# First loads in halves on two queues, V of chunk 0 alone, and 1/std spread by products: one core, one kernel of attention and a gated MLP

## The chip, the cores and the metric

The kernel runs on 1 core of one Trainium2 chip. The metric is device time in microseconds (us) of one execution; lower is better. Every time below is a median of several executions, all of the fast state unless one is named. The profile is taken in one of these executions; its span is 1.7 to 2.1 us shorter than the time.

In the text, *step 0, 1, 2* are the first turns of the attention loop, *chunk 0 to 3* are the first four blocks of 128 tokens (together segment 0), *x0 to x3* their loads, and *PE* is the tensor engine. *Fills* are products of later projections that the kernel puts between the logits of a step. *Gates* are sigmoid(beta) for each head; the *mask* is made from them on GpSimd. A *row* of WV is 128 of its 1024 rows, what one product uses.

## The reference, cut to what matters

```python
x = A_x                                        # 2048 tokens x 1024, bf16
h = x + _A_ref(_layernorm(x), wq, wk, wv, wo, beta)   # 32 heads, 4 segments of 512 tokens
h2 = h + _B_ref(_layernorm(h), w_in, w_sp, b_sp, w_out)

# in _A_ref, for each segment s of 512 tokens:
q, k, v = x @ wq, x @ wk, x @ wv
a_dot = softmax(q k^T * scale + mask) v        # inside the segment
num, den = phi(q) @ M, phi(q) @ z              # memory of the segments before (none for s = 0)
o = g * num / den + (1 - g) * a_dot            # g = sigmoid(beta)
M, z = M + phi(k)^T v, z + sum(phi(k))
```

Only the start of `_A_ref` for segment 0 is touched: layer norm of chunks 0 to 3, their transposes, and the first Q, K and V.

## The kernel before

All engines run their own list of instructions in program order; a recorder puts semaphores where data depend on each other. For segment 0 the kernel centres each chunk (x minus its mean), transposes it on the PE, and applies 1/std only to the outputs: as a scale per partition for V, and as a row over all tokens (`RB`) for Q and K.

```python
for k in range(8):                       # all on SP: x0, x1, WV 0-1, x2, WV 2-3, x3, WV 4-5, WV 6-7
    if k in (0, 1, 3, 5): x_load((k + 1) // 2)
    else: ...                            # two rows of WV[0], 256 KB
sp.dma_start(WK[:, :, 0:256], ...)       # then beta, WQ[:, :, 0:256], WV[1]
...
act.activation(RDM[:, 0, 0:1], MHALF[:], ACTF.Exp)      # makes the table load happen early
dve.tensor_single_scalar(IDENT[:], IOT[:], 0.0, ALU.is_equal)
...
warm(9)                                  # 9 products of IDENT and zeros, to raise the PE's clock
act_mean(1)                              # ScalarE: Copy with accumulation
var0(ln_stats(XCH[0]))                   # VectorE: statistics of chunk 0
c0 = center(0, MV[0][:, 0:1], ALU.subtract)
c1 = center(1, MEAN[1][:])
pe_Th(0, c0, dve, dve); pe_Th(1, c1, act, dve)          # 8 transposes each, and the copies out
... # (cut) V of chunks 0 and 1 together, rows 0-3; chunk 2; rows 4-7; chunk 3
diag(0); v_out(0, 0, 0, vb[0]); diag(1); diag(2); diag(3)   # 1/std on diagonals, in two bf16 parts
v_out(0, 1, 0, vb[1])
proj_v(0, 2, 0)                          # V of chunk 2
gates(); mask_g()                        # sigmoid(beta), and a mask of it on GpSimd
bk, bq, br = next_bank(), next_bank(), next_bank()
mm8(bank(bk), WK..., XNT[0]...)          # K of step 0
for i in range(2):                       # a ones matrix times the diagonals: the row of 1/std
    pe.matmul(bank(br), ONES[:], DIAG[i][:]..., start=(i == 0), stop=(i == 1))
act.activation(RB[:], bank(br), ACTF.Copy)
qk_out(0, 1, bk)
mm8(bank(bq), WQ..., XNT[0]...)          # Q of step 0
qk_out(0, 0, bq)
for tc in range(4, 8): x_load(tc)
sp.dma_start(WK[:, :, 256:D], ...); sp.dma_start(WQ[:, :, 256:D], ...)
```

The softmax here doesn't subtract the row's maximum and nothing guards it: scores larger than these inputs give would overflow.

## Time and profile before

| | before |
|---|---|
| time, median of the first 3 executions | 796.65 us |
| span of the profile (an execution of 797.13) | 795.1 us |
| PE busy | 789.9 us, 99% |
| transposes of chunk 0 start | 6.10 us |
| V of chunk 2 starts | 12.31 us |
| first logits (step 0) start | 19.75 us |
| Q of step 2 starts | 30.11 us |

The page of the kernel before: busy time of each engine, and the chain that ended last.

```profile
PE 789.9 (99%) x5657; PEld 378.4 (48%) x5657; DVE 379.3 (48%) x745; ACT 295.6 (37%) x347; POOL 172.1 (22%) x329
...
PE 96%; DMA 2%; DVE 1%; ACT 0%; SPq 0%; issue 0%
```

The PE is the limit nearly everywhere. From 30 us on it has no wait worth naming, so a change of the head can only move the moment at which the PE gets through its first products. The four milestones in the table are such moments; the work of the PE between them is the same before and after, but for the spreading of 1/std (0.44 us of the PE before, 0.46 after).

The PE's timeline of the kernel before. Columns: start, busy time, engine, line, operation, output<-inputs, shape, count, and in brackets the idle time just before with what ended it.

```profile
1.74 4.02 PE L209 MATMUL ps<-etmp,ident 128*128 128x512 bf16 x9 [1.74 <-DVE ident L209]
6.10 1.14 PE L209 MATMUL ps<-ident,lno 128*128 128x128 bf16 x16 [0.34 <-DVE lno L209]
7.09 0.39 PE L209 MATMUL ps<-wv,xnT 128*128 128x512 bf16 x1
7.71 1.68 PE L209 MATMUL ps<-wv,xnT 128*128 128x512 bf16 x7 [0.23 <-ACT xnT L209]
9.68 0.62 PE L209 MATMUL ps<-ident,lno 128*128 128x128 bf16 x8 [0.29 <-DVE lno L209]
...
12.31 1.89 PE L209 MATMUL ps<-wv,xnT 128*128 128x512 bf16 x8
...
19.75 0.40 PE L209 MATMUL ps<-qk 32*128 32x512 bf16 x4
```

How to read the speed from such lines: a group of n products takes (n - 1) spacings and one product's own length (for 512 columns 0.38 us at full speed, 0.63 at half). Seven V products in 1.68 us are 216 ns apart, full speed. The nine warm-up products in 4.02 us are 427 ns apart, half speed. The Trainium skill, "TensorE: Matmul & The Clock Gate" (Part 1), says that the PE starts at half its clock and gets the full clock after about 3.4 us of activity, as judged in a free-running window of that length; the trace agrees with the two spacings, 427 and 216 ns. The warm-up is there for this: it ends at 5.76, 0.34 us before the first transposes, and V runs at full speed.

### The profile page before, as it was taken

The page shows a single profiled execution, that of the slowest core. Times are in us where ns is not written, and L with a number is a line of the kernel's source. Part 1 is how long each engine was busy: PE and PEld are TensorE (multiplying, and loading weights), DVE is VectorE, ACT ScalarE, POOL GpSimd, SP SyncE. Part 2 cuts the span into 40 slices and gives each one's busy share as a digit, 9 for nine tenths or more (in the row PEclk, how much of TensorE's full clock was granted, in tenths as well). Part 3 has the DMA queues.
Part 4 walks back from the last instruction along what each step waited for, and adds up shares of the span by engine and source line. Part 5 has one row for each costly group of instructions (what it writes and reads, how often), then busy time and mean ns, then how long its engine had stood idle before and what let it go on. Part 6 is the DMA issues. An engine that isn't in the chain of part 4 may idle for free.

```text
span 795.1 us, 13111 instructions
## 1 busy us (share of the span) xinstructions
PE 789.9 (99%) x5657; PEld 378.4 (48%) x5657; DVE 379.3 (48%) x745; ACT 295.6 (37%) x347; POOL 172.1 (22%) x329
## 2 busy tenths in 40 slices
PE   8999999999999999999999999999999999999998
PEld 3445455554554455455544444444444444444444
DVE  7664689679854766744562000053234323323332
ACT  5777877887787675133333333100000000000000
POOL 4564565565553331100230000000000000000000
DMA  9862555363415325411116000740270043011002
GB/s 292 181 162 57 94 81 121 87 105 84 107 23 125 114 67 139 121 47 54 54 54 132 1 1 0 222 90 7 79 133 1 33 109 78 1 59 54 1 7 86
DMA packets 125002, 64.83 MB, mean 82 GB/s; under 512 B 94992, under 2 KB 113936, under 8 KB 124944
## 3 DMA queue, kind: packets, MB, share of 16 engines
q1 hardware_dynamic: 124944, 63.99, 33.7%
q8 instruction: 44, 0.72, 0.4%
q14 instruction: 14, 0.11, 0.1%
HBM read 32.51 MB, written 8.39 MB: 51 GB/s over the span
## 4 chain that ended last, share of the span: by engine, by line
PE 96%; DMA 2%; DVE 1%; ACT 0%; SPq 0%; issue 0%
PE ps L209 96%; DMA wq<-in_A_wq_dram 2%; DMA xch<-in_A_x_dram 0%; DVE stats L209 0%; ACT junk L209 0%; DVE xnT L209 0%; DVE lno L209 0%; SPq L209 0%; ACT xnT L209 0%; DVE mv L209 0%; DVE fin L209 0%
## 5 line engine op out<-in xcount | busy, mean ns | idle before, releaser
L209 PE MATMUL ps<-wspT,z 128*128 128x512 bf16 x896 | 194.0, 379 | 0.0
L209 ACT ACTIVATE e<-ps 128x2048 bf16<-128x2048 f32 (+1 forms) x96 | 152.6, 1590 | 41.9 <-PE ps L209 41.8
L209 PEld LDWEIGHTS ps<-wspT,z 128*128 128x128 bf16 x896 | 87.7, 98 | 105.7
L209 DVE TENSOR_TENSOR tmpg<-ps,brow 128x512 f32<-128x512 f32 x56 | 38.7, 691 | 196.7 <-DMA brow<-in_B_b_sp_dram 104.0
L209 POOL TENSOR_SCALAR_AFFINE_SELECT e<-e 128x512 bf16<-128x512 bf16 x128 | 90.4, 718 | 127.2 <-ACT e L209 127.1
L209 PE MATMUL ps<-win,hnT 128*128 128x448 bf16 x512 | 98.3, 352 | 0.0
L209 PE MATMUL ps<-w_out,yT 128*128 128x512 bf16 (+2 forms) x462 | 97.4, 373 | 0.0
L209 PE MATMUL ps<-hnT,win 128*128 128x512 bf16 x448 | 96.9, 379 | 0.0
L209 PEld LDWEIGHTS ps<-win,hnT 128*128 128x128 bf16 x512 | 49.7, 98 | 46.4 <-issue 0.2
L209 PEld LDWEIGHTS ps<-w_out,yT 128*128 128x128 bf16 x462 | 44.7, 98 | 52.3
L209 PEld LDWEIGHTS ps<-hnT,win 128*128 128x128 bf16 x448 | 43.8, 98 | 52.8
L209 PE MATMUL ps<-xnT,wk 128*128 128x512 bf16 x256 | 60.8, 380 | 0.0
L209 PE MATMUL ps<-xnT,wq 128*128 128x512 bf16 x256 | 60.6, 379 | 0.1
L209 PE MATMUL ps<-wv,xnT 128*128 128x512 bf16 x256 | 59.4, 380 | 0.2 <-ACT xnT L209 0.2
L209 ACT ACTIVATE z<-ps 128x448 bf16<-128x448 f32 x60 | 32.5, 543 | 69.4 <-PE ps L209 69.4
L209 PE MATMUL ps<-wo,oT 128*128 128x512 bf16 x256 | 58.0, 379 | 0.0
L209 ACT ACTIVATE z1T<-ps 128x512 bf16<-128x512 f32 x56 | 33.4, 597 | 63.3 <-PE ps L209 63.3
L209 DVE TENSOR_TENSOR fin<-fin,ps 128x512 bf16<-128x512 bf16 (+2 forms) x33 | 22.2, 671 | 71.2 <-DMA fin<-out_dram 39.7
L209 DVE BATCH_NORM_STATS2 zst<-z 128x6 f32<-128x448 bf16 x64 | 38.9, 619 | 30.1 <-ACT z L209 30.1
L209 PEld LDWEIGHTS ps<-v,e 128*128 128x128 bf16 x1280 | 38.8, 96 | 14.0 <-issue 6.5
L209 PE MATMUL ps<-v,e 128*128 128x33 bf16 x1280 | 42.2, 178 | 0.0
L209 DVE TENSOR_TENSOR yT<-tmpg,z1T 128x512 bf16<-128x512 f32 x56 | 38.8, 692 | 1.9
(86 smaller groups left out, 609.3 us busy)
## 6 DMA issues: line engine op xcount, KB each, us to landing
xch<-in_A_x_dram SPq DMA_DIRECT2D x16, 256.0 KB, 3.3
xr<-in_A_x_dram SPq DMA_DIRECT2D x16, 256.0 KB, 3.7
out_dram<-hch SPq DMA_DIRECT2D x16, 256.0 KB, 2.4
fin<-out_dram SPq DMA_DIRECT2D x16, 256.0 KB, 2.8
out_dram<-fin SPq DMA_DIRECT2D x31, 128.0 KB, 1.7
win<-in_B_w_in_dram SPq DMA_DIRECT2D x4, 896.0 KB, 5.1
w_out<-in_B_w_out_dram SPq DMA_DIRECT2D x1, 3584.0 KB, 12.7
win<-in_B_w_in_dram SPq DMA_DIRECT2D x3, 1024.0 KB, 5.2
```

The source lines that it names most:

```text
L209: ins = getattr(e, op.name)(*op.args, **op.kw)
```

## The change

Its intent: get the PE to work on chunk 0 sooner. x0 and x1 are loaded in halves, one half by SP and one by ScalarE's queue, in step with single rows of WV. The mean of chunk 0 is taken in two halves on two engines. V of chunk 0 runs alone instead of in pairs with chunk 1. The diagonals on VectorE go; the row of 1/std comes from eight small products whose stationary operand is one column of 1/std repeated with step 0. The warm-up no longer waits for the identity. Gates and mask move behind Q and K of step 0, and the fills of step 0 are rearranged; one background piece of layer norm in step 2 (`bg_pop`) also moves behind a fill, which the cut below leaves out.

```diff
-    for k in range(8):  ... (all on SP, whole chunks; see above)
+    for kind, k in (("x", 0), ("w", 0), ("w", 2), ("x", 1), ("w", 4), ("w", 6)):
+        for h, eng in ((0, sp), (1, act)):
+            if kind == "x":
+                x_half(k, h, eng)            # 128 KB
+            else:
+                wv_row(k + h, eng)           # 128 KB
+    x_load(2)
+    x_load(3)
...
-            pe.matmul(bank(7), IDENT[:], ETMP[:, 0, :], start=True, stop=True)
+            pe.matmul(bank(7), ETMP[:, 0, 0:128], ETMP[:, 0, :], start=True, stop=True)
...
-    warm(9)
-    act_mean(1)
-    var0(ln_stats(XCH[0]))
...
+    warm(8)
+    act_half(0)                              # ScalarE: half of the sum
+    dve_half(0)                              # VectorE: the other half, and both together
+    center_half(0, 0)
+    center_half(0, 1)
+    pe_Th(0, LNO[0], dve, dve)
+    act_mean(1)
+    v_pair(0, 0, 6)                          # V of chunk 0 alone
...
+    stats0(0, 0)  ... act_var(1) ... act_var(2) ... stats0(3, 0) ...   # statistics later
+    dve.tensor_copy(RSB[:, 0, :], RSW[:, :, 0])
+    dve.tensor_tensor(RSB[:, 1, :], RSW[:, :, 0], RSB[:, 0, :], ALU.subtract)
...
-    gates()
-    mask_g()
...
-        pe.matmul(bank(br), ONES[:], DIAG[i][:].rearrange("p c n -> p (c n)"), start=(i == 0), stop=(i == 1))
+    for t in range(4):
+        for h in range(2):
+            pe.matmul(PS[:, br, t * 128:(t + 1) * 128], RSB[:, h, t:t + 1].to_broadcast([128, 128]), IDENT[:],
+                      start=(h == 0), stop=(h == 1))
...
+    gates()
+    mask_g()
```

## The prediction

> **What bounds the kernel.** The page gives the tensor engine (PE) 789.9 of 795.1 us busy, and the chain of waits is 96% PE. In the PE timeline the first warm-up product starts at 1.74 us and the last product ends near 792.8, so all PE gaps sum to about 1.2 us. From 30 to 140 us no PE group waits 0.15 us. The change touches only the first 30 us, so it can gain only earlier first logits (19.75 us now) plus those gaps: a ceiling of about 1.5 us, 0.2%.
>
> **What the head looks like now** (timeline, landings in the trace). x0 lands at 3.83, x1 4.45, x2 7.42, x3 8.80 us; pairs of WV rows at 6.08, 8.12, 9.54, 10.32. Chunk 0 pays two statistics reads (1.42), an aggregate (0.21) and a centring (0.49), so its transposes start at 6.10. From 7.7 the PE runs almost solid: gaps of 0.23 us and 0.29 us.
>
> **Costs of the change.**
> - Chunk 0's mean: half a Copy with accumulation on ScalarE (whole one 1.06 + 0.19; a half about 0.63 + 0.19) beside a half reduction on VectorE (est. 0.6), a tiny combine (0.2), one half-centring (0.27): about 1.4 us from landing to first transpose instead of 2.25, a possible 0.8 us.
> - Against it: ScalarE must issue six DMAs (0.43-0.47 us each on SP's queue, 2.7 us) beside its table load (1.28). Serial, ScalarE is free only at 0.8 + 2.7 + 1.3 + 0.2 = 5.0 us and transposes start near 6.1, no gain; overlapped, near 4.9.
> - x1 moves behind four WV rows, x2 and x3 to the very end. x1 becomes the end of the first 1 MB (was 512 KB): about 6.2-7.2, x3 about 9.3-10.3. ScalarE's means are serial (1.25 each), so chunk 3's transposes cannot start before x3 + 1.25 + 0.45 + 0.1, or 11.1-12.1; now 11.86. This likely eats the early start.
> - Two queues: rate dips to 234-300 GB/s between 3.5 and 7 us, against 350-385 later. The Trainium skill ("DMA: Bandwidth & Descriptors", Issuing engines are not separate DMA queues) says a second issuer saves only issue time; the dip leaves room for about 1 us at most.
> - Spreading 1/std: eight 0.60-us-per-pair VectorE diagonal operations vanish (2.4 us of VectorE, off the critical path); two 512-column products (0.43 us) become eight 128-column ones (est. 8 x 0.06 = 0.5): zero or slightly worse for PE.
> - Gates and their mask move about 3.4 us later on GpSimd (5.8 us of work, now 16.5 to 22.3, then to about 25.7); four selects then end near 28.4, just when the first value products (28.4) need them: little or nothing.
>
> **Sum.** Chunk 2's value products, now from 12.31 us, start at 11.7-12.6; PE work from there to the first logits is unchanged (7.35 us needed, 7.44 taken). Net -0.5 us, from -1.4 to +0.4.
>
> **Predicted:** 796.1 us, 8 in 10 between 795.2 and 797.0. Faster by over 2%: 0.005; within 2%: 0.99; slower by over 2%: 0.005.
>
> **What would show it.** Right: span about 794.6, PE busy share still 99%, first transposes at 4.9-6.1, a PE wait for chunk 1 or 2 data between 6 and 11 us, logits of step 0 at 19.0-20.0, the same spacing after 30 us. The supply step is wrong if x3 lands before 9 us; the ScalarE step is wrong if its first half-mean starts before 4.
>
> **What would make it wrong.** The PE staying at the cold spacing (427 ns per 512 columns) after a shorter warm-up; a mask on GpSimd arriving late and stalling the first value products.

## More of the kernel before

One more line of before, from VectorE's timeline, is needed later: the add of phi of K in step 0.

```profile
18.73 0.28 DVE L209 TENSOR_SCALAR pqk<-qk 128x512 bf16<-128x512 bf16 x1
```

## The result

| | before | after |
|---|---|---|
| time, median of 6 executions each | 796.70 us | 798.86 us |
| span of the profile | 795.1 us | 797.1 us |
| PE busy | 789.9 us | 790.8 us |
| transposes of chunk 0 start | 6.10 | 6.47 |
| transposes of chunk 2 start | 9.68 | 12.10 |
| V of chunk 2 starts | 12.31 | 13.86 |
| first logits start | 19.75 | 21.77 |
| Q of step 2 starts | 30.11 | 32.25 |

The ratio of the times is 1.0029 with a 95% interval of 1.0016 to 1.0042. Ratios here are the mean time of one kernel's fast runs over that of the other's of the same rounds, so not quite the ratio of the medians quoted. The change costs about 2.2 us: small, within 2%, but clear of noise and outside the predicted range.

The milestones say where. 1.55 us are lost ahead of V of chunk 2; 0.47 more up to the first logits (7.91 us instead of 7.44 from V of chunk 2); 0.12 more up to Q of step 2 (10.48 instead of 10.36; the changed kernel loses 0.59 us there, shown below, but the kernel before also lost time there that the changed one does not, mainly 0.28 us ahead of Q of step 2 for the load of WQ). The difference of the spans is 2.0 us. Nothing is lost after about 25 us.

Two cautions. First, the profile of before is one of its slower executions (797.13 us). In g2 below, whose head is that of before, the profile is of a usual one (796.45): there x2 landed at 6.28 instead of 7.42, V of chunk 2 starts at 11.93 and the first logits at 19.36. Against that the head of the changed kernel loses 1.93 us and 2.41 us, not 1.55 and 2.02. Second, time minus span is 2.0 to 2.1 us in every execution of before, f3 and g2 whose span is on record, and 1.7 to 1.8 in every such execution of the kernels with the new spreading, f2 too. So about 0.3 us change outside the span, where no timeline shows them; no run says why.

The page of the changed kernel, the same two lines:

```profile
PE 790.8 (99%) x5662; PEld 378.3 (47%) x5662; DVE 378.8 (48%) x741; ACT 296.3 (37%) x349; POOL 170.0 (21%) x328
...
PE 97%; DVE 1%; ACT 1%; POOL 0%; ACTq 0%; issue 0%; DVEq 0%
```

These whole-kernel numbers say almost nothing about the loss; PE's busy share is 99% in both. The PE's timeline of the changed kernel does:

```profile
1.24 3.37 PE L209 MATMUL ps<-etmp 128*128 128x512 bf16 x8 [1.24 <-DVE etmp L209]
6.47 0.66 PE L209 MATMUL ps<-ident,lno 128*128 128x128 bf16 x8 [1.86 <-DVE lno L209]
7.38 2.51 PE L209 MATMUL ps<-wv,xnT 128*128 128x512 bf16 x6 [0.26 <-DVE xnT L209]
9.69 1.06 PE L209 MATMUL ps<-ident,lno 128*128 128x128 bf16 x8
...
12.10 0.61 PE L209 MATMUL ps<-ident,lno 128*128 128x128 bf16 x8
...
13.86 1.89 PE L209 MATMUL ps<-wv,xnT 128*128 128x512 bf16 x8
...
18.63 0.62 PE L209 MATMUL ps<-ident,rsb 128*128 128x128 bf16 x8 [0.29 <-DVE rsb L209]
...
21.77 0.40 PE L209 MATMUL ps<-qk 32*128 32x512 bf16 x4
22.10 1.90 PE L209 MATMUL ps<-wv,xnT 128*128 128x512 bf16 x8
24.42 0.61 PE L209 MATMUL ps<-xnT,wq 128*128 128x512 bf16 x2 [0.41 <-DVE qk L209]
```

Four things are to be seen. First, the PE idles 1.86 us between the warm-up and the first transposes. Second, the six V products from 7.38 take 2.51 us, where at full speed they would take 1.46 (5 x 0.216 + 0.38), and the eight transposes from 9.69 take 1.06 us instead of 0.61: the PE has fallen back to half speed, from about 7.6 to 11.0 us by the starts of the products. Such a group shows no idle time and counts as busy; only its length for its count gives it away. (The last warm-up product was already short, so the full clock had come at about 4.2 us.) Third, there is a wait of 0.29 us for the new 1/std columns. Fourth, there is one of 0.41 us for an output of K, ahead of Q of step 1.

Why chunk 0 is late is in ScalarE's timeline of the changed kernel (ACTq is its queue of loads):

```profile
0.79 0.40 ACTq L209 DMA_DIRECT2D xch<-in_A_x_dram  x1
...
2.67 0.94 ACTq L209 DMA_DIRECT2D wv<-in_A_wv_dram  x2
3.64 1.28 ACT L209 ACT_TABLE_LOAD   x1 [3.64 <-issue]
4.93 0.20 ACT L209 ACTIVATE rdm<-mhalf 128x1 f32<-128x1 f32 x1
5.04 0.61 ACT L209 ACTIVATE junk<-xch 128x512 bf16<-128x512 bf16 x1
...
9.97 1.06 ACT L209 ACTIVATE junk<-xch 128x1024 bf16<-128x1024 bf16 x1 [1.50 <-DMA xch<-in_A_x_dram]
```

ScalarE issues its six loads until 3.6 us, and only then does its first activation bring the table load, 1.28 us (the Trainium skill, "ScalarE: Activation LUTs", What ACT_TABLE_LOAD costs, states about 1283 ns; the trace agrees). The half mean of chunk 0 starts at 5.04, 1.2 us after both halves are there. The last line shows the supply side: chunk 2's mean starts when x2 lands, at 9.97; before, it started at 7.55.

The fourth wait shows on VectorE and GpSimd in the changed kernel's timeline:

```profile
21.75 1.05 POOL L209 COPY maskg<-gs 128x1024 f32<-128x1024 f32 x1 [3.57 <-DVE gs L209]
...
21.81 1.13 DVE L209 TENSOR_SCALAR pqk<-qk 128x512 bf16<-128x512 bf16 x1
```

The add of phi of K takes 1.13 us instead of 0.28, and it ends 0.14 us after GpSimd's copy ends. The Trainium skill, "SBUF — State Buffer" (Who interferes with whom), says that VectorE in its fast modes and GpSimd hold one pair of ports exclusively and the later one is blocked for the whole instruction. The trace fits: the later one was VectorE's add. With the gates moved, VectorE makes this add just when the mask's first copy runs.

### The profile page after: what moved, and what is told of

Read it like the earlier page. It is cut to its first block, busy times and chain, and to the rows that moved or that the text cites. A ratio compares the mean times of both kernels' runs of the same rounds, so it can differ in the third digit from the quotient of the medians.

```text
span 797.1 us, 13128 instructions
## 1 busy us (share of the span) xinstructions
PE 790.8 (99%) x5662; PEld 378.3 (47%) x5662; DVE 378.8 (48%) x741; ACT 296.3 (37%) x349; POOL 170.0 (21%) x328
## 4 chain that ended last, share of the span: by engine, by line
PE 97%; DVE 1%; ACT 1%; POOL 0%; ACTq 0%; issue 0%; DVEq 0%
PE ps L209 97%; ACTq L209 0%; POOL rsw L209 0%; DVE qk L209 0%; ACT junk L209 0%; DVE pqk L209 0%; ACT L209 0%; POOL rs L209 0%; ACT rb L209 0%; ACT xnT L209 0%; DVE gs L209 0%; DVE xnT L209 0%; DVE lno L209 0%; DVE rsb L209 0%; DVE fin L209 0%
```

## The experiments

The theory after the result: (A) ScalarE's late start lets the PE idle, and this costs it its full clock; (B) x2 and x3 now land late; (C) the statistics and 1/std come late; (D) the late gates block VectorE. The rivals: all of the first part is supply, or the order of V, or the step-0 operand is slow. Each batch of kernels ran on one chip with runs of the kernel before beside it; the ratios are against these. Each ratio has an interval of about 0.0012, or 1 us, to either side, and the changed kernel itself came at 798.86 us in its first batch and at 798.45 in a later one (r1). Smaller differences between two repaired kernels are therefore read from the milestones in the traces, one profile each, and not from the times. (Expectations for e1 and its batch name 6.77 us and 7.9 to 11.4 us; I had read these with a zero 0.3 us too late. In the profile they are 6.47 and 7.6 to 11.0.)

### e1: fourteen warm-up products

```diff
-    warm(8)
+    warm(14)
```

> The changed kernel with 14 warm-up products instead of 8, so that the PE is fed until the first transposes (6.77 us). Clock theory: the half-speed stretch seen from 7.9 to 11.4 us (427 ns between 512-column products) vanishes; chunk 2's transposes start near 11.7 instead of 12.10, V of chunk 2 near 13.4 instead of 13.86, time 0.3 to 0.6 us under the changed kernel's 798.86. Supply theory (ScalarE free at 5.0, x1 at 7.25, x2 at 9.89, x3 at 10.60 us set the pace alone): spacing becomes 216 ns but V of chunk 2 stays within 0.15 us of 13.86 and the time within 0.2 us.

Measured: 797.85 us (before beside it: 796.56), ratio 1.0012, 1.0 us under the changed kernel's first batch and so more than I expected. V of chunk 2 at 12.99 instead of 13.86. The warm-up stayed at half speed, lasted to about 7.2 and pushed the first transposes from 6.47 back to 7.19, and still the head ended 0.87 us sooner, because every product after it was 216 ns apart. This speaks for the clock, but x2 landed 0.6 us earlier in this profile than in the changed kernel's, so the size was not settled; r1 and r2 below settle it.

### e2: the loads of before

```diff
-    for kind, k in (("x", 0), ("w", 0), ("w", 2), ("x", 1), ("w", 4), ("w", 6)): ...
-    x_load(2)
-    x_load(3)
+    for k in range(8): ...                   # as before: all on SP, x1 second
```

> The changed kernel with the loads of before: whole chunks, one queue (SP), x1 before the WV rows; everything else of the change stays. Supply theory: ScalarE starts its half mean at x0's landing (3.8) instead of 5.04, transposes of chunk 0 start near 5.0, V of chunk 2 near 12.0 to 12.4 (now 13.86), and 1.3 to 1.9 us come back: about 797.2. If the order of V (chunk 0 alone) is what costs: V of chunk 2 stays after 13.2 and under 0.7 us comes back. The waits after it (0.4 for 1/std, 0.4 for the late mask) should stay if they are not consequences of the late start.

Measured: 797.91 us where about 797.2 was expected, ratio 1.0020; one of its six executions took 800.94. Transposes at 5.03, no half-speed stretch, V of chunk 2 at 12.83: better than the change, not as good as expected. The PE's timeline of e2 shows the new wait:

```profile
7.18 0.60 PE L209 MATMUL ps<-wv,xnT 128*128 128x512 bf16 x2 [0.64 <-DMA wv<-in_A_wv_dram]
8.68 0.59 PE L209 MATMUL ps<-wv,xnT 128*128 128x512 bf16 x2 [0.89 <-DMA wv<-in_A_wv_dram]
```

V of chunk 0 alone eats rows of WV twice as fast as the pair of chunks does, and with the old order of loads it waits for them. So the new order of loads and V of chunk 0 alone belong together; neither can be judged without the other. The two later waits (0.29 and 0.41 us) stayed, as expected.

### e3: the table load first

```diff
+    pool.memset(MHALF[:], -0.5)
+    act.activation(RDM[:, 0, 0:1], MHALF[:], ACTF.Exp)
     for kind, k in (("x", 0), ("w", 0), ...        # the loads; the two lines above moved up from below
```

> The changed kernel with the warm-up Exp (and so its table load) issued on ScalarE ahead of its six loads. If the table load and the issues overlap: table load at 0.8 to 2.1, the loads issued in the same time, half mean at 3.8, transposes of chunk 0 near 5.0 to 5.3 instead of 6.47, the PE idle under 0.5 us before them, no half-speed stretch; time 0.4 to 0.8 us under 798.86. If they are serial whatever the order: ScalarE's first load is issued only near 2.2, x0 lands near 5, nothing gained (within 0.2 us).

Measured: 798.01 us, ratio 1.0014, 0.85 us under the change's first batch and 0.44 under r1, which ran on the same chip. ScalarE's timeline of e3:

```profile
0.79 1.28 ACT L209 ACT_TABLE_LOAD   x1 [0.79 <-PEq L970]
0.93 0.38 ACTq L209 DMA_DIRECT2D xch<-in_A_x_dram  x1
...
3.77 0.63 ACT L209 ACTIVATE junk<-xch 128x512 bf16<-128x512 bf16 x1 [1.48 <-DMA xch<-in_A_x_dram]
```

Table load and issues overlap when the load comes first. The half mean starts at 3.77, the transposes at 5.21, no product after them is at half speed, and V of chunk 2 starts at 12.50. With one line moved, most of the first loss is gone in this profile; x2 also landed 1.0 us earlier in it than in the changed kernel's first (8.92 against 9.89), which the table under r1 and r2 takes apart. The 0.3 and 0.4 us waits stayed.

### e4: the gates back

```diff
+    gates()
+    mask_g()
     bq, br, bk = 5, 6, 7
     ...
-    gates()
-    mask_g()
```

> The changed kernel with the gates and their mask back ahead of K of step 0, as before the change. Gates theory: GpSimd does the mask from about 16.5 to 22.5 instead of 21.75 to 27.3; the add for phi of K (1.04 us on VectorE in the changed kernel, 0.28 before) is short again, the 0.41 us PE wait ahead of Q of step 1 (24.42 us) vanishes, time 0.3 to 0.5 us lower. Rival (the wait is from the order of the step-0 fills): the wait stays and the time is within 0.15 us. The three gate operations of VectorE in front of the 1/std rows could cost up to 0.3 us at the spreading instead.

Measured: 798.18 us, ratio 1.0018. The wait ahead of Q of step 1 is gone (PE's timeline of e4):

```profile
22.03 1.90 PE L209 MATMUL ps<-wv,xnT 128*128 128x512 bf16 x8
23.76 0.59 PE L209 MATMUL ps<-xnT,wq 128*128 128x512 bf16 x2
```

From V to Q are 1.73 us, where the change took 2.32 (22.10 to 24.42): 0.59 us. The phi add fell from 1.13 to 0.52 us. V of chunk 2 (13.77) and the wait for 1/std (0.31) stayed. Theory D holds.

### f1: three repairs in the changed kernel

The table load first, the gates back, and chunk 0's statistics right after its copies, where VectorE is idle:

```diff
     pe_Th(0, LNO[0], dve, dve)
+    stats0(0, 0)
+    stats0(0, 1)
+    aggr0(0)
     act_mean(1)
```

> The changed kernel with three repairs at once: the table load ahead of ScalarE's loads, the gates back ahead of K of step 0, and VectorE's statistics of chunk 0 done in its idle time after chunk 0's copies instead of behind chunk 3's centring. If the loss is the sum of these waits: no half-speed stretch, V of chunk 2 near 12.5, the idle PE before the spreading products 0 to 0.1 us instead of 0.29, no wait before Q of step 1; the first logits near 20.0 to 20.2 (21.77 in the changed kernel, 19.75 before) and the time about 796.4 to 797.0, level with before. If something else in the change costs (the order of the loads, the step-0 fills): over 797.4.

Measured: 796.92 us (before beside it: 796.58), ratio 1.0005 with an interval of 0.9992 to 1.0017: level with before. First logits at 20.41 rather than the hoped 20.0 to 20.2; no half-speed stretch and no wait ahead of Q of step 1. The wait for 1/std became smaller but did not vanish: from the first product of Q of step 0 to the spreading are 1.10 us (16.16 to 17.26), in the changed kernel 1.32 (17.31 to 18.63), where four products take 0.86. By the times these waits make up about 1.8 of the 2.2 us. In the profile less is mended: the first logits are still 0.66 us later than in the profile of before, and V of chunk 2 came near 12.7 (its first product is missing from the trace) instead of 12.5. Part of the early start is spent on loads: the PE idled 0.68 us ahead of the fifth V product, whose row of WV landed at 7.71, and 0.56 us ahead of chunk 1's transposes (the second half of x1 landed at 7.19). No gain is shown for what remains of the change.

### f2: only the new spreading, in the kernel before

```diff
-    diag(0) ... diag(3);  pe.matmul(bank(br), ONES[:], DIAG[i][:]...)
+    (two small VectorE operations; eight products with RSB[:, h, t:t + 1].to_broadcast([128, 128]))
```

> The kernel before with only the new spreading of 1/std (eight 128-column products with a stationary operand of step 0, two small VectorE operations, no diagonals). Theory: the products with step 0 cost no more than others (56 ns apart, weight loads of 98 ns) and the spreading can start a little earlier, as the pair of diagonal operations behind the last 1/std (0.6 us) becomes 0.35 us: first logits 0.05 to 0.25 us earlier than 19.75, time within 0.3 us of before. Rival (the step-0 operand loads slowly or small products cost much): over 100 ns apart, first logits 0.3 us or more later.

Measured: 796.26 us, ratio 0.9998 (0.9986 to 1.0011). PE's and PEld's lines for the new operand in f2:

```profile
L209 PEld LDWEIGHTS ps<-ident,rsb x8: 97/98/98, 15.1 to 15.7; 128*128 128x128 bf16 x8
L209 PE MATMUL ps<-ident,rsb x8: 219/219/219, 15.4 to 15.7; 128*128 128x128 bf16 x8
```

The columns in the middle are least, median and greatest duration in ns. A weight load from one repeated column takes 98 ns like any other, and the eight products take 0.61 us as a group, as eight transposes do. From K to Q of step 0 are 2.17 us, before 2.16. The first logits came at 19.35, but in this profile the transposes of chunk 0 also started earlier, at 5.76; in g2, which starts at 5.79 and keeps the old spreading, the first logits came at 19.36. So the hoped 0.05 to 0.25 us did not come. Inside the span the spreading is neutral, and the rival of a slow step-0 operand falls.

### f3: only the late gates, in the kernel before

```diff
-    gates()
-    mask_g()
     ...
     qk_out(0, 0, bq)
+    gates()
+    mask_g()
```

> The kernel before with only the gates and their mask moved behind the outputs of Q and K of step 0, as the change has them. Theory: the mask on GpSimd then runs beside VectorE's phi of K, whose add grows from 0.28 to about 1.0 us, and K of step 1 is taken out of its bank late; before, Q of step 1 follows a whole V and the same banks, so 0.3 to 0.6 us are lost between the first logits and 28.4 us: time 0.2 to 0.6 us over before. Rival (the move only hurts together with the new step-0 fills): within 0.15 us of before.

Measured: 797.08 us against 796.58, ratio 1.0005 with an interval of 0.9992 to 1.0019, so not clear by time. In the profile the phi add takes 1.13 us here too, and from the first logits to K of step 2 are 7.15 us instead of 6.92. The block on VectorE comes with the move alone; how much of it reaches the PE depends on the fills (0.59 us in the new ones, about 0.2 in the old).

### f4 and g1: a mix of both kernels

f4 takes the loads of before, the half means of the change, V by pairs of rows as WV lands, statistics in idle time, early gates and the new spreading. The core of the edit to the changed kernel:

```diff
-    v_pair(0, 0, 6)  ... v_pair(0, 6, 8) ... v_pair(1, 0, 4) ... v_pair(1, 4, 8)
+    v_pair(0, 0, 2); (chunk 1's transposes); v_pair(1, 0, 2); v_pair(0, 2, 4); v_pair(1, 2, 4)
+    (chunk 2's transposes); v_pair(0, 4, 6); v_pair(1, 4, 6); (chunk 3's); v_pair(0, 6, 8); v_pair(1, 6, 8)
```

> A new mix: the loads of before (one queue, x1 ahead of the WV rows), chunk 0's mean in two halves as in the change, the V products of chunks 0 and 1 row pair by row pair in the order in which WV lands, the statistics in idle time, gates early, the new spreading. Theory (ScalarE's late start, the supply order and V of chunk 0 alone were the losses, the half means and the spreading are sound): transposes of chunk 0 near 5.0, V of chunk 2 at 11.6 to 12.1 (12.31 before), first logits at 19.0 to 19.5, time 0.3 to 0.9 us under before. If it is not under before, the half means buy nothing because WV's landing (last pair near 10.3) sets the pace.

Measured: 796.22 us, ratio 0.9997 (0.9984 to 1.0009). The head came out as expected (transposes at 4.96, first logits at 19.35), but PE's timeline of f4 shows where it was given back:

```profile
30.46 1.67 PE L209 MATMUL ps<-xnT,wq 128*128 128x512 bf16 x7 [1.08 <-DMA wq<-in_A_wq_dram]
```

(Seven of the eight products are in the trace. If the first is the missing one, the wait was about 0.87 us.) Q of step 2 needs columns of WQ that come in the last of the early loads, and in this profile these landed at 30.11 us, although the PE was early. In the kernel before, Q of step 2 started at 30.11, right after the same load. g1 splits these loads:

```diff
-    for tc in range(4, 8): x_load(tc)
-    sp.dma_start(WK[:, :, 256:D], ...); sp.dma_start(WQ[:, :, 256:D], ...)
+    sp.dma_start(WK[:, :, 256:512], ...); sp.dma_start(WQ[:, :, 256:512], ...)
+    for tc in range(4, 8): x_load(tc)
+    sp.dma_start(WK[:, :, 512:D], ...); sp.dma_start(WQ[:, :, 512:D], ...)
```

> The mix of f4 with the rest of WK and WQ loaded in two parts: columns 256 to 511 of each ahead of chunks 4 to 7 of x, the other half behind them. In f4 the PE waited 1.08 us for the end of the WQ load (landed 30.1 us) before Q of step 2. Theory: that wait was the only place where f4's early start was given back; it vanishes, Q of step 2 starts near 29.4, span near 794.0, time 0.7 to 1.3 us under before. Rival (other waits take its place, as the same bytes must land by then): time no better than f4's 796.22.

Measured: 796.10 us, before beside it 796.52, ratio 0.9991 (0.9979 to 1.0004). The wait is gone, Q of step 2 starts at 29.13, the span is 794.0: as foreseen. The time gained is 0.4 us by the medians, half of what I expected, and 0.7 by the ratio; about 0.3 of it lies outside the span. All five executions (795.66 to 796.27) lie below all nine of before (796.34 to 797.34), but the interval still touches 1. I had compared with the profile of before, an execution of 797.13; its usual execution is about 0.6 us faster.

### g2: the same split in the kernel before

The edit is the split of g1, and nothing else.

> The kernel before with only the same split of the later WK and WQ loads. Its Q of step 2 starts at 30.11, right when the WQ load lands (30.06). Theory: 0.1 to 0.3 us come back; this is also the amount that hides part of any loss or gain of the head in before. Rival: within 0.1 us.

Measured: 796.45 us, ratio 1.0001: nothing, so the rival holds. In its profile Q of step 2 starts at 29.45. In before, the WQ load is only in the way in some executions: in f2, with the same later loads as before, it landed at 28.32 and nothing waited for it.

### g3: f1 with all first loads on one queue

```diff
-        for h, eng in ((0, sp), (1, act)):
+        for h, eng in ((0, sp), (1, sp)):
```

> f1 with its first loads in the same order and sizes, but all issued by SP instead of half by ScalarE. If two queues only save issue time: SP needs 16 issues of 0.45 us (7 us), so x2 and x3 are issued near 6 us and land at most 0.5 to 1.5 us later than in f1 (9.1 and 9.9 us); chunk 0's halves land within 0.5 us of f1; the time is within 0 to 0.8 us above f1's 796.92. If two queues do not matter at all: within 0.2 us. If two queues raise the rate of the first MB: x1 lands over 1 us later than 7.2.

Measured: 798.69 us, 1.8 us over f1 (on another chip; 2.0 by the two ratios to before), ratio 1.0030: far outside what I expected. SP's timeline of g3:

```profile
3.61 0.91 SPq L209 DMA_DIRECT2D xch<-in_A_x_dram  x2
4.56 1.85 SPq L209 DMA_DIRECT2D wv<-in_A_wv_dram  x4
6.45 0.91 SPq L209 DMA_DIRECT2D xch<-in_A_x_dram  x2
```

One issue takes 0.46 us, and with 131,072 bytes each that caps a single queue at about 285 GB/s, an estimate (131,072 bytes over 0.46 us). x2 and x3 are issued only at 6.45, and in this profile, which fell on a slow execution (800.75; the others took 798.4 to 798.9), the PE waited 2.89 us for chunk 2 (x2 landed at 11.56, in f1 at 9.13) and then ran at half speed again, from about 13.9 to 17.3. x1 landed at 6.30 and 6.64, no later than in f1 (6.99 and 7.19), so two queues are not shown to raise the rate of the first loads. So halves need the second queue. It does not follow that halves on two queues beat whole chunks on one: with those, in before, x3 landed at 8.80 and the last WV pair at 10.32; after the change the last WV row landed at 9.17 and x3 at 10.60.

### r1 and r2: the changed kernel again, and eleven warm-up products

r1 has no edit. r2:

```diff
-    warm(8)
+    warm(11)
```

> The changed kernel itself once more, beside the next one on the same chip, to see what of its head repeats. Expected if the half-speed stretch belongs to the kernel: 3 us or more of products spaced 427 ns (512 columns) or 107 ns (128 columns) after the first transposes again, V of chunk 2 at 13.6 to 14.0, time 798.3 to 799. If the stretch of the first profile was luck of that run: products 216 ns apart from 7.4 us on, V of chunk 2 near 13.2. Whole chunk 2's landing, 9.89 in the first profile, tells how much of the start of V is load luck.

> The changed kernel with 11 warm-up products: at 427 ns they end at 5.9, 0.5 us before the first transposes, so that unlike 14 they don't push them back. Clock theory: no half-speed products after about 7.6 us, chunk 0's transposes at 6.47, V of chunk 2 0.4 to 0.9 us earlier than in the run of the changed kernel beside it, time 0.3 to 1.0 us under it. If the gain of e1 was only load luck (its chunk 2 landed 0.6 us earlier): no difference in time (within 0.2 us).

Measured: r1 798.45 us, r2 798.06 us by the medians; by the ratios to the same runs of before 1.0023 and 1.0014, which are 0.0009 of 797 us or 0.7 us apart. The intervals (1.0011 to 1.0036 and 1.0000 to 1.0027) overlap, so the times alone do not settle it; the timelines do. PE's timeline of r1:

```profile
1.24 3.59 PE L209 MATMUL ps<-etmp 128*128 128x512 bf16 x8 [1.24 <-DVE etmp L209]
6.49 1.03 PE L209 MATMUL ps<-ident,lno 128*128 128x128 bf16 x8 [1.65 <-DVE lno L209]
7.62 2.74 PE L209 MATMUL ps<-wv,xnT 128*128 128x512 bf16 x6
10.15 0.78 PE L209 MATMUL ps<-ident,lno 128*128 128x128 bf16 x8
...
12.10 0.61 PE L209 MATMUL ps<-ident,lno 128*128 128x128 bf16 x8
...
13.86 1.89 PE L209 MATMUL ps<-wv,xnT 128*128 128x512 bf16 x8
```

and of r2:

```profile
1.25 4.07 PE L209 MATMUL ps<-etmp 128*128 128x512 bf16 x11 [1.25 <-DVE etmp L209]
6.48 0.66 PE L209 MATMUL ps<-ident,lno 128*128 128x128 bf16 x8 [1.16 <-DVE lno L209]
7.40 1.47 PE L209 MATMUL ps<-wv,xnT 128*128 128x512 bf16 x6 [0.26 <-DVE xnT L209]
...
11.31 0.62 PE L209 MATMUL ps<-ident,lno 128*128 128x128 bf16 x8
...
13.08 1.89 PE L209 MATMUL ps<-wv,xnT 128*128 128x512 bf16 x8
```

This pair is the decisive one. In r1 x2 landed 1.3 us earlier than in the first profile (8.55 against 9.89), and V of chunk 2 started at 13.86 all the same, because the PE was at half speed from 6.49 to about 10.5 and was busy nearly all that time. In r2 x2 landed late (9.50) and V of chunk 2 started at 13.08. Supply alone would have it the other way round. It is one profile each, but the half speed shows in all three profiles with eight warm-up products and late transposes (after, r1, e4) and in neither with more (e1, r2).

The rule behind it: ScalarE takes chunk 2's mean (1.06 and 0.19 us), VectorE centres it (0.49), and with the hand-overs chunk 2's transposes start 1.81 us after x2's landing in both r2 and e3, where the PE is ready before.

| kernel | x2 landed | + 1.81 | transposes of chunk 2 | V of chunk 2 | half speed after the transposes |
|---|---|---|---|---|---|
| after | 9.89 | 11.70 | 12.10 | 13.86 | 7.6 to 11.0 |
| r1 (the same) | 8.55 | 10.36 | 12.10 | 13.86 | 6.5 to 10.5 |
| e4 (gates back) | 9.71 | 11.52 | 12.01 | 13.77 | 6.5 to 10.3 |
| r2 (11 warm-ups) | 9.50 | 11.31 | 11.31 | 13.08 | none |
| e1 (14 warm-ups) | 9.28 | 11.09 | 11.23 | 12.99 | none |
| e3 (table load first) | 8.92 | 10.73 | 10.73 | 12.50 | none |

With the full clock the supply of x2 sets the pace in r2 and e3; in e1, whose warm-up pushed the transposes back, the PE came 0.14 us after it. With the half clock the PE sets it. In all cases V of chunk 2 follows 1.76 or 1.77 us later. (Landings are read from the trace's record of each load's completion; starts from the PE's timeline.)

## Why the prediction was wrong

It said 796.1 us (795.2 to 797.0) and the result was 798.86. Point by point:

- *That the PE bounds the kernel, that only the first 30 us matter, and that at most 1.5 us can be gained*: right as far as the runs show; none gained more.
- *Serial, ScalarE is free only at 5.0 us*: right, 5.04. The transposes followed at 6.47 rather than 6.1, and the prediction left open whether the table load would overlap the issues. It does if it comes first (e3).
- **The step that failed: "Chunk 2's value products, now from 12.31 us, start at 11.7-12.6."** They started at 13.86. The sum left out the clock. The prediction named "the PE staying at the cold spacing (427 ns per 512 columns) after a shorter warm-up" as a risk and gave it no time in the sum. It had both numbers that should have raised it: its serial case has transposes near 6.1, and eight warm-up products that wait for nothing but a memset end near 4.6. An idle gap of 1.5 us behind a shorter warm-up follows from the two. r1 and r2 show its price in their profiles, 0.78 us (13.86 to 13.08). In the changed kernel's first profile it is smaller: there x2 landed so late (9.89) that chunk 2's transposes could have started at 11.70 by the rule above, 0.40 before they did. So of the 1.55 us the clock cost 0.4 to 0.8, depending on when x2 lands, and by the same rule the late x2 makes up most of the rest. With r2's landing, of the other 0.77 us, 0.58 is the step from r2 to e3, in which x2's landing is also 0.58 us earlier; 0.19 remains between e3 and the profile of before (0.57 against g2).
- *The supply step*, "x3 about 9.3-10.3", chunk 3's transposes from 11.1 to 12.1: too kind. x3 landed at 10.60 and these transposes started at 13.41; the formula counted one mean after x3, but x2's mean, the copies of chunk 2 and the PE's order come between.
- *"PE work from there to the first logits is unchanged (7.35 us needed, 7.44 taken)"*: the work was, the time was not: 7.91. The prediction costed the spreading as products and did not follow the chain ahead of it: the statistics were moved late, GpSimd's last small operation for 1/std ended at 18.18 and VectorE's two at 18.57, while the PE was ready at 18.17 (17.31 and four products of 0.216). In g1, whose statistics come earlier, the spreading follows without a wait (15.24 to 16.11, 0.87 us). The cost of the products themselves was right (f2).
- *The late gates, "little or nothing"*: 0.59 us in the new fills (e4). The prediction watched the selects on GpSimd and missed that GpSimd's first copy would block VectorE's phi add.

What is open: the landing of x2 differed by over 1 us between executions of the same kernel (8.55 and 9.89), and no run here shows why. By its time f1 stands at the level of before, so the half means and V of chunk 0 alone were neither shown to gain nor to lose once the waits are gone. g1 is about 0.4 us better than before by its medians, with an interval that touches 1. Also open are the 0.3 us outside the span.

## What to carry to other kernels

A warm-up is measured by where it ends, not by its count: when you shorten or advance it, check the gap to the first real product, and read the clock from the spacing of products, as half speed counts as busy. An engine that is given loads to issue starts its own work later; put its table load ahead of them, so that the two overlap. When you move small work out of one place, follow the whole chain that ends in the next product, and ask what the moved operation will run beside on a shared port.

## What the Trainium skill lacked or had wrong

- "TensorE: Matmul & The Clock Gate" advises no idle gaps over about 3 us between bursts. Here an idle gap of 1.65 to 1.86 us behind 3.4 to 3.6 us of warm-up was enough: the full clock came and went (after) or did not come until about 10.5 us (r1). With 1.16 us of idle behind 4.07 us (r2) it came and stayed; in g3, 2.89 us of idle were followed by half speed too. Its remark that clock records can't be fully trusted agrees: the granted clock is given as 0.77 for 5 to 10 us of the changed kernel, but as 1.00 for the same stretch of r1, whose products were 427 ns apart for longer.
- "DMA: Bandwidth & Descriptors" says that a second issuing engine only saves issue time, usually small beside the transfer. With loads of 128 KB it is not small: 0.46 us each, and one queue instead of two cost 1.8 us by the medians (g3 against f1).
- "ScalarE: Activation LUTs" states a drain of about 1.38 us beside the table load of 1.28. No such drain shows here: the next activation started 0.01 us after the first load (3.64 + 1.28 to 4.93); the load for the gelu started 0.02 us after the activation before it ended (300.40 + 1.02 to 301.44), and the next one 0.02 us after that load (301.44 + 1.28 to 302.74, in the kernel before). No page tells that the table load runs beside load issues of the same engine if it stands first, 0.79 to 2.07 us in e3.
- "SBUF — State Buffer" had the port lock right: a VectorE add of 0.28 us took 1.13 beside a GpSimd copy of 1.05.
